# Complex-decay attention ahead of two dense layers: the angle sums and the steps that use them, one slot later

## The chip, the cores and the metric

The kernel runs on one core of a Trainium2 chip. The metric is the device time of one execution in microseconds (us). Before the change it is 1105.33 us, the median of three runs (1104.63 to 1105.64). The core has TensorE (PE in the profile, its weight loads PEld), VectorE (DVE), ScalarE (ACT), GpSimd (POOL) and SyncE (SP), which issues most of the DMAs. Each engine works through its own queue in order.

## The reference

Three stages. The first is a linear attention with a complex decay over 4 batches, 8 heads, 768 steps and head size 48:

```python
mag = sqrt(a_re**2 + a_im**2); a = (a_re + 1j*a_im) * minimum(mag, 0.999) / (mag + 1e-6)
for t in range(768):                                # per batch and head
    S = a[t][:, None] * S + outer(k[t], v[t])       # complex state, real k and v
    y[t] = q[t] @ S.real
```

Then `x = y` as 3072 rows of 384; `h = x @ w_in` (to 2048 columns), `g = h * tanh(softplus(h))`, `x = g @ w_out`; and `out = ((x @ w_a) * (x @ w_b)) @ w_out2` with 1536 columns inside.

## The kernel before

The kernel works in blocks: block j holds the 128 time steps j*128 to j*128+127 of all four batches, that is 512 rows, so there are 6 blocks. The attention works in chunks: chunk c = 4*j + b is 128 steps of one batch with all 8 heads, 24 chunks in all. Chunks 0 to 3 are done in a lead-in of their own. The attention of the later ones is threaded through the first dense stage: while block j goes through `w_in` and `w_out`, the chunks of block j+1 are prepared, so that no attention is left for block 5 and none for the second dense stage.

**The dense work around it.** Lines 913 and following run over units (block, f) with 16 values of f a block. A unit is: nine matmuls into `hps` (`moe1_h`, L594); one or more attention slots; the first half of the activation (`mish_factor`: VectorE L600, then four ScalarE steps on tile `m`, recorded at the helper's L59); nine matmuls of the unit two back into three `x2ps` banks (`moe1_x2`, L637; in block 0 three slower ones on unsplit numbers); one or more slots again; and `mish_product` (VectorE L614, L620, GpSimd L621), which also frees the `hps` bank. There are two `hps` banks, so the `hps` of a unit needs the L614 of the unit two back. From block 2 to block 4 there are 32 slots for the 32 half-units of a block, one each; in block 0 there are 43 and in block 1 there are 44, so some half-units hold two.

**The slots.** Chunk c has its first slot at `slot_0(c)`, 8 slots after that of chunk c-1 (20 after it at chunk 8). The lists `early` and `late` (L551 to L562) give each step a slot relative to it; within a slot the steps with the larger relative number, those of the chunk in front, are written first, and `trig`, `angle` and `decay_exp` ahead of all. So slot 6 of chunk c is also slot 14 of chunk c-1. The steps that matter here, by relative slot:

- 4: `carry` (L302) and `split_theta` (L309): the angles of the chunk get the turn carried over from the chunk four back, and are split into a high part `sh` (GpSimd L316) and a low part `sl` (VectorE L320).
- 5: `sum_ell` (L323): the running sum over time of the logarithms of the decay, a product with a triangular matrix, in a PSUM bank `pl`.
- 6: `sum_theta` (L323, matmuls at L329): the same for the angles, in a bank `pt`, two matmuls; and `decay_exp` (L343): two exponentials on ScalarE that read `pl` (out tile `size`).
- 7: `reduce_angle` (L349): VectorE reads `pt` twice (L353, L354) and works once more on the result in SBUF (L355); `hand_turn` (L359) and `hand_end` (L364) issue a DMA each on SP that carries the chunk's last row to the chunk four later; `scale_qk` (L381).
- 11: `trig`, sine and cosine of the reduced angles on ScalarE; 12: `rotate`.
- 14 and 15: `transposes` (L422) of the first and of the last four heads: four transposes of the queries into a bank `pqT`, four of the keys into `pkT` (L410), each copied out by ScalarE (`qT`, `kT`).
- 16: `scores` (L441): eight heads of products into two banks `psc` (L433), copied with the causal mask by VectorE (L439, `am`); 17: `values` (L445, bank `py`, L463), `outer` (bank `pu`) and `state`.

**The banks.** `pl`, `pqT`, `pkT`, `pt`, `psc`, `py` and `pu` of these chunks share the three PSUM banks of the pool `ps_a` (L116), so each of them needs that the bank of the third one in front, in the order in which they are written, has been read. The order of the ten is: `pl`; `pqT`, `pkT` (first heads, chunk c-1); `pt` (chunk c); `pqT`, `pkT` (last heads, chunk c-1); `psc`, `psc`, `py`, `pu` (chunk c-1). So `pt` takes the bank that `decay_exp` frees.

**The order on an engine.** The program is written in the order above, but the framework places an instruction behind later written ones where its own plan says that it isn't ready yet; the order in the trace is the one that it chose.

Of the kernel before, what the change touches and what calls it, by code (L numbers as in the profile page):

```python
# [21 lines left out]
def kernel(  # L22
# [524 lines left out]
    def slot_0(c):  # L547
# [3 lines left out]
    early = [  # L551
        (-4, load_a), (0, decay_1), (1, decay_2), (1, decay_3), (2, tangent), (2, decay_4), (3, angle),
        (3, split_ell),
        (4, carry), (4, split_theta), (5, sum_ell), (6, sum_theta), (6, decay_exp), (7, reduce_angle),
        (7, hand_turn), (7, hand_end), (7, scale_qk), (11, trig),
    ]
    late = [
        (10, read_end), (11, load_v), (14, lambda c: transposes(c, 0)), (15, lambda c: transposes(c, 1)),
# [597 lines left out]
```

## Time and profile before

| | us |
|---|---|
| median of three runs | 1105.33 (1104.63 to 1105.64) |
| the profiled execution | 1105.48 |
| its span, from the first to the last instruction | 1103.8 |
| PE busy / DVE busy / ACT busy / POOL busy | 1052.8 / 655.9 / 613.8 / 230.0 |

The span is one execution as the hardware profiler recorded it; the rest of the profiled time, 1.7 us, lies around it. A row of a timeline gives start, duration, engine, line, operation, the tile written and the tiles read, the shapes, and in brackets how long the engine had been idle and what ended that. The ends of matmuls are modelled and overlap the next one; the rate of a stretch of matmuls is read from their starts. The attention of chunks 4 to 23 lies between about 60 and 560 us; what follows is dense work alone.

### The profile page before, as it was taken

The page shows a single profiled execution, that of the slowest core. Times are in us where ns is not written, and L with a number is a line of the kernel's source. Part 1 is how long each engine was busy: PE and PEld are TensorE (multiplying, and loading weights), DVE is VectorE, ACT ScalarE, POOL GpSimd, SP SyncE. Part 2 cuts the span into 40 slices and gives each one's busy share as a digit, 9 for nine tenths or more (in the row PEclk, how much of TensorE's full clock was granted, in tenths as well). Part 3 has the DMA queues.
Part 4 walks back from the last instruction along what each step waited for, and adds up shares of the span by engine and source line. Part 5 has one row for each costly group of instructions (what it writes and reads, how often), then busy time and mean ns, then how long its engine had stood idle before and what let it go on. Part 6 is the DMA issues. An engine that isn't in the chain of part 4 may idle for free.

```text
span 1103.8 us, 15912 instructions
## 1 busy us (share of the span) xinstructions
PE 1052.8 (95%) x6060; PEld 875.5 (79%) x6060; DVE 655.9 (59%) x998; ACT 613.8 (56%) x968; POOL 230.0 (21%) x265
## 2 busy tenths in 40 slices
PE   4989989999999999999999999999999999999997
PEld 2856656878887888888777878888888888888886
DVE  6799965787677677676669998641322322322222
ACT  8868876898788887778767853221222212221211
POOL 2012343343334434433331122200000000000000
PEclk9999999999999999999999999999999999999999
DMA  9548752353534343343145457210000100100000
GB/s 203 107 138 197 176 150 61 70 94 74 121 67 86 72 94 66 68 113 79 44 114 179 140 187 226 85 58 1 29 30 1 53 5 1 43 1 1 29 1 31
DMA packets 203549, 90.92 MB, mean 82 GB/s; under 512 B 144781, under 2 KB 187850, under 8 KB 203466
## 3 DMA queue, kind: packets, MB, share of 16 engines
q1 hardware_dynamic: 202410, 89.62, 32.9%
q8 instruction: 50, 0.82, 0.3%
q10 hardware_dynamic: 1056, 0.21, 0.1%
q14 instruction: 33, 0.27, 0.1%
HBM read 72.44 MB, written 17.36 MB: 81 GB/s over the span
## 4 chain that ended last, share of the span: by engine, by line
PE 67%; DVE 13%; ACT 9%; issue 5%; DMA 3%; POOL 2%; SPq 1%; ACTq 0%; DVEq 0%; POOLq 0%
PE ops L717 12%; PE psa L692 12%; PE psb L692 12%; PE x2ps L637 11%; PE hps L594 10%; ACT m L59 4%; PE psc L433 3%; PE py L463 3%; ACT L54 2%; DVE m L600 1%; PE pu L502 1%; PE pkT L410 1%; PE pqT L410 1%; DVE wf L168 1%; DVE wf L169 1%
## 5 line engine op out<-in xcount | busy, mean ns | idle before, releaser
L703 DVE TENSOR_TENSOR a_sb<-a_sb,psb 128x512 f32<-128x512 f32 x72 | 49.3, 685 | 225.0 <-PE psb L692 225.0
L59 ACT ACTIVATE m<-m 128x512 f32<-128x512 f32 x192 | 119.9, 630 | 74.4 <-DVE m L600 63.6
L59 ACT ACTIVATE a_sb<-psa 128x512 f32<-128x512 f32 x72 | 42.9, 595 | 161.5 <-PE psa L692 159.4
L59 ACT ACTIVATE ph<-a_sb 128x512 fp32r<-128x512 f32 x72 | 45.4, 631 | 156.8 <-DVE a_sb L703 156.8
L594 PE MATMUL hps<-xh,winh 128*128 128x512 f32 x288 | 119.2, 415 | 6.3 <-DVE gh L611 5.2
L621 POOL TENSOR_TENSOR gl<-m,gh 128x512 fp32r<-128x512 f32 x64 | 82.9, 1295 | 157.6 <-DVE gh L620 146.0
L594 PE MATMUL hps<-xl,winh 128*128 128x512 f32 x288 | 113.4, 394 | 0.0
L594 PE MATMUL hps<-xh,winl 128*128 128x512 f32 x288 | 113.1, 393 | 0.0
L717 PE MATMUL ops<-woh,ph 128*128 128x384 f32 x288 | 97.2, 337 | 0.0
L717 PE MATMUL ops<-woh,pl 128*128 128x384 f32 x288 | 97.2, 337 | 0.0
L637 PE MATMUL x2ps<-gl,wouth 128*128 128x512 f32 x240 | 94.6, 394 | 2.3 <-DVE gl L621 1.3
L717 PE MATMUL ops<-wol,ph 128*128 128x384 f32 x288 | 96.8, 336 | 0.0
L637 PE MATMUL x2ps<-gh,wouth 128*128 128x512 f32 x240 | 93.8, 404 | 1.8 <-ACT gh L59 1.5
L637 PE MATMUL x2ps<-gh,woutl 128*128 128x512 f32 x240 | 94.0, 392 | 0.0
L614 DVE SCALAR_TENSOR_TENSOR m<-m,hps 128x512 f32<-128x512 f32 x80 | 54.5, 682 | 61.5 <-ACT m L59 61.2
L692 PE MATMUL psa<-xh,wal 128*128 128x512 f32 x216 | 85.2, 395 | 0.0
L692 PE MATMUL psa<-xl,wah 128*128 128x512 f32 x216 | 85.1, 394 | 0.0
L692 PE MATMUL psa<-xh,wah 128*128 128x512 f32 x216 | 84.4, 391 | 0.4 <-DVE a_sb L703 0.4
L692 PE MATMUL psb<-xh,wbh 128*128 128x512 f32 x216 | 84.3, 390 | 0.0
L692 PE MATMUL psb<-xh,wbl 128*128 128x512 f32 x216 | 84.2, 390 | 0.0
L692 PE MATMUL psb<-xl,wbh 128*128 128x512 f32 x216 | 84.2, 390 | 0.0
L600 DVE TENSOR_SCALAR m<-hps 128x512 f32<-128x512 f32 x96 | 65.4, 682 | 17.0 <-PE hps L594 16.7
(167 smaller groups left out, 2324.3 us busy)
## 6 DMA issues: line engine op xcount, KB each, us to landing
wraw<-in_moe_w_out_dram SPq DMA_DIRECT2D x14, 768.0 KB
wraw<-in_moe_w_in_dram SPq DMA_DIRECT2D x8, 768.0 KB
a<-in_a_re_dram SPq DMA_DIRECT2D x24, 192.0 KB
q<-in_q_dram SPq DMA_DIRECT2D x24, 192.0 KB
k<-in_k_dram SPq DMA_DIRECT2D x24, 192.0 KB
v<-in_v_dram SPq DMA_DIRECT2D x24, 192.0 KB
wraw<-in_moe_w_a_dram SPq DMA_DIRECT2D x6, 768.0 KB
wraw<-in_moe_w_b_dram SPq DMA_DIRECT2D x6, 768.0 KB
```

The lines of the kernel that those rows point to most:

```text
L54: load = nc.scalar.preload_act_table_set(name)
L59: x = nc.scalar.activation(**kw)
L433: nc.tensor.matmul(p[:, i, :], lhsT=st["kT", c, hf][:, i, :], rhs=st["qT", c, hf][:, i, :], start=True, stop=True)
L463: nc.tensor.matmul(p[par * 64:(par + 1) * 64, i, :], lhsT=w[:, col:col + 64], rhs=x[:, first + par, :], start=(n == 0), stop=(n == len(ter ...
L594: nc.tensor.matmul(p, lhsT=w[:, kk, :], rhs=x[:, kk, :], start=(i == 0), stop=(i == len(ops) - 1))
L600: nc.vector.tensor_scalar(m, p, 20.0, None, ALU.min)
L614: nc.vector.scalar_tensor_tensor(m, m, 2.5, p, ALU.subtract, ALU.mult)
L621: (nc.vector if on_act else nc.gpsimd).tensor_tensor(gl, m, gh.bitcast(F32), ALU.subtract)
L637: nc.tensor.matmul(x2ps[m], lhsT=w[:, ms], rhs=x, start=(f == 0 and i == 0), stop=(f == NF - 1 and i == len(terms) - 1),)
L692: nc.tensor.matmul(p, lhsT=w[:, kk, :], rhs=x[:, kk, :], start=(i == 0), stop=(i == len(ops) - 1))
L703: nc.vector.tensor_tensor(a_sb, a_sb, pb, ALU.mult)
L717: nc.tensor.matmul(ops_t[t], lhsT=x[:, tsl], rhs=w, start=(f == 0 and i == 0), stop=(f == NF2 - 1 and i == 2),)
```

## The change

Three numbers in the list `early`: `sum_theta` goes from slot 6 to slot 7, `reduce_angle` and `hand_turn` go from slot 7 to slot 8. No instruction is added, removed or altered.

```diff
     early = [
         (-4, load_a), (0, decay_1), (1, decay_2), (1, decay_3), (2, tangent), (2, decay_4), (3, angle),
         (3, split_ell),
-        (4, carry), (4, split_theta), (5, sum_ell), (6, sum_theta), (6, decay_exp), (7, reduce_angle),
-        (7, hand_turn), (7, hand_end), (7, scale_qk), (11, trig),
+        (4, carry), (4, split_theta), (5, sum_ell), (7, sum_theta), (6, decay_exp), (8, reduce_angle),
+        (8, hand_turn), (7, hand_end), (7, scale_qk), (11, trig),
     ]
```

As written, the angle sums of chunk c then stand behind the second transposes of chunk c-1, in front of the next unit's `hps`, and `reduce_angle` and `hand_turn` stand behind the `scores` of chunk c-1. The order of the ten banks becomes `pl`, `pqT`, `pkT`, `pqT`, `pkT`, `pt`, `psc`, `psc`, `py`, `pu`: `pt` now takes the bank of the first `pkT`, and `py` takes the bank of `pt`. The chunks of the lead-in are not touched, since their order is written out apart.

## Rows read from the trace of the kernel before

**Rows 1.** The page's first part: busy time of TensorE.
```profile
PE 1052.8 (95%) x6060; PEld 875.5 (79%) x6060; DVE 655.9 (59%) x998; ACT 613.8 (56%) x968; POOL 230.0 (21%) x265
```
**Rows 2.** Busy time by stretch: PE, PEld, DVE, ACT, POOL, then clock, DMA share, GB/s.
```profile
60.00:130.00 70.00, 63.07 (x440) 42.80 (x439) 67.20 (x100) 55.93 (x88) 14.39 (x16) 1.00 0.68 183
292.00:504.00 212.00, 208.06 (x1462) 173.78 (x1458) 151.36 (x242) 170.41 (x269) 82.09 (x100) 1.00 0.39 85
```
**Rows 3.** Waits of PE: whole span, then 300 to 510: us, times, longest.
```profile
PE pt L329 <- ACT size L59: 6.2, 12, 1.1
...
PE pt L329 <- ACT size L59: 3.9, 9, 0.5
```
**Rows 4.** Timeline of PE, slots 6 to 9 of chunk 16.
```profile
355.39 0.63 PE L410 MATMUL pkT<-ident,khp 128*128 128x128 f32 x4
355.77 0.48 PE L637 MATMUL x2ps<-gh,wouth 128*128 128x512 f32 x1
356.73 0.41 PE L329 MATMUL pt<-sh,csum_r 128*128 128x384 f32 x1 [0.48 <-ACT size L59]
...
357.31 0.39 PE L637 MATMUL x2ps<-gl,wouth 128*128 128x512 f32 x1
...
359.92 0.48 PE L594 MATMUL hps<-xh,winh 128*128 128x512 f32 x1
...
362.07 1.95 PE L433 MATMUL psc<-qT,kT 128*128 128x128 f32 x16
...
366.02 0.44 PE L463 MATMUL py<-qT,W 128*64 128x128 f32 x4
```
**Rows 5.** The same of chunks 14, 22 and 23: first key transposes, next hps.
```profile
305.85 0.63 PE L410 MATMUL pkT<-ident,khp 128*128 128x128 f32 x4
...
310.39 0.48 PE L594 MATMUL hps<-xh,winh 128*128 128x512 f32 x1
...
503.21 0.63 PE L410 MATMUL pkT<-ident,khp 128*128 128x128 f32 x4
...
507.75 0.48 PE L594 MATMUL hps<-xh,winh 128*128 128x512 f32 x1
...
527.62 0.63 PE L410 MATMUL pkT<-ident,khp 128*128 128x128 f32 x4 [0.24 <-DVE khp L395]
...
532.40 0.48 PE L594 MATMUL hps<-xh,winh 128*128 128x512 f32 x1
```
**Rows 6.** The same behind the last chunk, where no angle sums follow.
```profile
551.33 0.63 PE L410 MATMUL pkT<-ident,khp 128*128 128x128 f32 x4
...
554.67 0.47 PE L594 MATMUL hps<-xh,winh 128*128 128x512 f32 x1
```
**Rows 7.** Timeline of PE, chunk 11: angle sums between transposes and hps.
```profile
243.81 0.42 PE L329 MATMUL pt<-sh,csum_r 128*128 128x384 f32 x1
...
244.25 0.39 PE L594 MATMUL hps<-xh,winh 128*128 128x512 f32 x1
```
**Rows 8.** Timeline of ACT, slots 6 and 7 of chunk 16.
```profile
357.57 0.63 ACT L59 ACTIVATE m<-m 128x512 f32<-128x512 f32 x1
358.09 0.60 ACT L59 ACTIVATE kT<-pkT 128x512 f32<-128x512 f32 x1
```
**Rows 9.** Timeline of DVE, slots 6 to 8 of chunk 16.
```profile
357.51 0.56 DVE L353 TENSOR_SCALAR a<-pt 128x384 f32<-128x384 f32 x1 [0.54 <-PE pt L329]
358.10 0.56 DVE L354 TENSOR_TENSOR a<-pt,a 128x384 f32<-128x384 f32 x1
...
359.17 1.08 DVE L355 TENSOR_SCALAR a<-a 128x384 uint32<-128x384 uint32 x1
...
362.10 0.69 DVE L614 SCALAR_TENSOR_TENSOR m<-m,hps 128x512 f32<-128x512 f32 x1 [1.52 <-ACT m L59]
...
363.64 1.36 DVE L439 COPY_PREDICATED am<-csum,psc 128x512 f32<-128x512 int32 x2
```
**Rows 10.** Line 355 from 300 to 510: duration in ns, min/median/max.
```profile
L355 DVE TENSOR_SCALAR a<-a x9: 352/1024/1196, 309.6 to 507.0; 128x384 uint32<-128x384 uint32 x9
```
**Rows 11.** Timeline of POOL beside it.
```profile
359.03 1.00 POOL L384 TENSOR_TENSOR k<-k,size 128x384 f32<-128x384 f32 x1 [0.73 <-DMA k<-in_k_dram]
```

## The prediction, made before the changed kernel ran

> **What bounds the kernel.** I began with the page's busy times: TensorE is busy for 1052.8 us of the span [rows 1], so whatever gives it time shortens the kernel and whatever another engine saves does not, unless TensorE waits for it. I then cut the time into stages. From 292 to 504 us, where the slots come one to a half-unit, TensorE is busy 208.06 of 212.00 us, and ScalarE (170.41) and VectorE (151.36) have room; from 60 to 130 us it is VectorE that is full, 67.20 of 70.00 us [rows 2]. Next I asked what TensorE waits for. The angle sums `pt` stand out: 12 waits, 6.2 us, all for the exponentials that read `pl`, and nine of them, 3.9 us, lie in the even stretch [rows 3]. That idle time is less than what is lost, because a matmul's modelled end covers the start of a gap. So I went to the timeline of one chunk [rows 4]: behind the first key transposes one x2 matmul starts at 355.77, the next thing to start is the angle sum at 356.73, and the second x2 matmul starts only at 357.31. An order that was written ahead of the whole x2 group was put behind its first matmul, and still came too early for ScalarE.
>
> **The sum, part by part.** I measure the stretch from the first key transposes to the next `hps`, because both orders hold the same work in it: four key transposes, nine x2 matmuls, two angle sums, eight second transposes.
>
> Now: 355.39 to 359.92 = 4.53 us [rows 4]; in the first of the nine 310.39 - 305.85 = 4.54, in the last 507.75 - 503.21 = 4.54 [rows 5]. The last chunk has its sums in the same place and is worse: 532.40 - 527.62 = 4.78 [rows 5].
>
> After: behind the last chunk the same stretch runs with no angle sums in it, 554.67 - 551.33 = 3.34 us [rows 6]. What two ready angle sums add between transposes and an `hps` is seen at chunk 11, where the framework happened to put them there: 244.25 - 243.81 = 0.44 us [rows 7]. Together 3.78 us.
>
> Gain: 9 x (4.53 - 3.78) = 6.75 us, and 4.78 - 3.78 = 1.00 us at the last chunk, 7.75 us in all. For this to stand, nothing else may become late by more than it has room. I take the users in the order in which TensorE meets them, at chunk 16, 0.75 us earlier than now:
>
> - The second transposes take the bank of `pl`, free before 356.73 [rows 4], and are reached over 1 us later. The keys among them take the bank of the first `pqT`, whose copy stands in front of that of `kT` on ScalarE. No cost.
> - The angle sums are reached at 355.39 + 3.34 = 358.73 and need the bank of the first `pkT`, copied from 358.09 to 358.69 [rows 8]. That is level. A wait of 0.1 us for each of ten would cost 1 us; none costs 0. I take 0, since the copy is over 0.04 us before, and keep 1 us for the range.
> - The next `hps` is reached at 358.73 + 0.44 = 359.17 and needs the L614 of the unit two back. Its last ScalarE step ends at 357.57 + 0.63 = 358.20 [rows 8]; with 0.69 us for L614 [rows 9] it is free at 358.89. Today L614 shares VectorE with the two reads of `pt` that stand before it. 0.28 us to spare.
> - `py` is reached at 366.02 - 0.75 = 365.27 [rows 4] and needs the masked copies, which end at 363.64 + 1.36 = 365.00 today [rows 9]. They stand behind an L614 that waits for ScalarE until 362.10, so they don't get earlier. 0.27 us to spare, if `reduce_angle` finds its place before 362.10. The angle sums end near 359.2; the reads take 0.56 + 0.56 [rows 9] and L355 0.35 to 1.20 [rows 10], so they are over by 361.5, inside the 1.52 us for which VectorE idles [rows 9] and the place that L355 has now. No cost.
> - `hand_turn` goes behind `hand_end` on SP and waits there for L354. Behind it on SP stand the read of the chunk's end values and the next chunk's carried turn. The first is used at slot 17, the second at the next chunk's slot 4, so a microsecond there is hidden; without that cover it would be one DMA wait a chunk. `trig` comes four slots behind the angle sums, and the split parts `sh` and `sl` are freed a slot later than now but wanted again only at slot 11. Both at no cost, hidden by those slots.
>
> **The uneven part** is chunks 4 to 13, in blocks 0 and 1. There the x2 groups, slots and waits do not repeat. Of the twelve waits nine are in the even stretch and one in the last chunk; the other two lie here and hold less than 6.2 - 3.9 = 2.3 us [rows 3]. In block 0 VectorE is full, so what TensorE gains it would wait off again. Bounds: a gain of 2.3 us, and a loss of the two reads, 1.1 us, at four chunks, 4.5 us. I take 0, as nothing is taken off or put on the full engine.
>
> The sum is made against the profiled execution, 1105.48 us: 1105.48 - 7.75 = 1097.7. The median of the runs is 0.15 lower, so I predict **1097.6 us**. Its own range, with the bounds above, is 1095 to 1103.
>
> **A rule that speaks against it.** L355 took 1.08 us at 359.17, beside a GpSimd product that ran from 359.03 to 360.03 [rows 9, 11], while the shortest of the nine took 0.35 [rows 10]. The Trainium skill, "SBUF — State Buffer", section "Who interferes with whom", says that VectorE and GpSimd share a port pair which one of them holds for a whole instruction while the other stands still. The trace agrees. By that rule the moved L355 could be made to wait for a whole GpSimd operation of the slot that it moves into, ahead of the masked copies; as an estimate that stays under the 1.20 us of the nine, so the sum would not change, but the third rival's chance rises.
>
> **The rivals.**
>
> 1. *The wait changes its place and stays as long.* The bank of `pkT`, the L614 and the masked copies all hang on ScalarE's steps, and the room is 0.0, 0.3 and 0.3 us. If ScalarE or VectorE has its steps in another order so that one of the three comes 0.75 us later, `py` starts at 366.02 again: 1105. For it: the small margins. Against: today's order of ScalarE doesn't depend on `pt` in this stretch, and each margin is counted with nothing moved forward. If half goes, the time is near 1101.5.
> 2. *The change does not do what it says.* The framework orders by its own plan, so the sums could land at a wrong place again. TensorE always has an `hps` or x2 matmul ready, though, and the sums are now written behind both the x2 group and the transposes, so they can't come in front of these unless those are not ready in its plan. 1105, a small chance.
> 3. *Slower: `reduce_angle` lands between the L614 of 362.10 and the masked copies.* It is written behind `scores`, and `py` now takes the bank of `pt` as well, so either way `py` waits for both. Price: 0.56 + 0.56 + 0.35 to 1.20 = 1.47 to 2.32 us behind 365.00, so `py` starts at 366.5 to 367.3, that is 0.45 to 1.3 us later than today, at ten chunks 4.5 to 13 us: 1110 to 1118, middle 1114. It decides as soon as the reads start behind 361 us on this clock. For it: the program order, and the margin of 0.27 us. Against: the sums are ready 2 us and more before the scores are, with VectorE idle in between.
>
> **The chances.** The forecast 0.62, half of it 0.08, no gain (rivals 1 and 2, the loss in the uneven part eating the gain) 0.14, slower 0.16. A measurement of this kernel tells 0.2%, about 2.2 us, from no change. Faster by more than that is 0.62 + 0.08 = 0.70, within it 0.14, slower 0.16. The range 1094 to 1107.5 holds the forecast, the half and no gain; most of rival 3 lies outside.
>
> **What would show it.** Right: in the changed trace the angle sums stand behind eight second transposes in chunks 14 to 23, with no wait for the exponentials; key transposes to `hps` takes some 3.8 us; `py` to `py` of neighbouring chunks falls by 0.75 us; L353 starts near 359.4 on this clock, before an L614. Wrong: the sums wait for the copy of `kT`; `py` waits for `am`; L353 stands behind that L614; or the even stretch gains and the time before 292 us loses as much.

## The result, and the profile after

The changed kernel takes **1092.31 us**, the median of four runs (1091.60 to 1092.88), beside 1104.98 us (1104.04 to 1105.64) for the kernel before on the same chip: a ratio of 0.989, 95% interval 0.9876 to 0.9905. It is 12.67 us faster, where 7.75 had been forecast, and ends below the low end of the range, which the prediction gives once as 1095 and once as 1094 us. Its profiled execution took 1092.23 us, with a span of 1090.4 us, 13.4 less than before.

Where the 13.4 us come from is read off the start of the first `py` matmul of a chunk (us from the start of the span), in the timelines of PE of both kernels:

| | before | after | gained since the row above |
|---|---|---|---|
| `py` of chunk 4 | 94.30 | 93.61 | 0.69 |
| `py` of chunk 7, the last prepared during block 0 | 167.90 | 162.89 | 4.32 |
| `py` of chunk 12 | 291.62 | 286.25 | 0.36 |
| `py` of chunk 23 | 560.77 | 547.48 | 7.92 |
| end of the span | 1103.8 | 1090.4 | 0.11 |

The last eleven chunks give 7.92 us, which is what the sum of 7.75 was about. The other 5.5 us were gained ahead of that nearly all, 5.0 of them by the end of block 0, for which the prediction had put down 0.

Not all of these 5.0 us are the change's. Before the first step that it moves, the angle sums of chunk 4 at about 60 us, the two profiles already lie apart: `pl` of that chunk starts at 60.12 us before and at 57.41 after. TensorE's granted clock was 0.66 from 50 to 60 us in the profile before, at the end of the lead-in, and 1.00 in the profile after. It is a matter of the single execution: the same kernel before, profiled once more (e0 below), kept its clock. The stretch in the first profile and in e0:

```profile
50.00:60.00 10.00, 10.00 (x65) 7.77 (x65) 8.38 (x14) 6.54 (x9) 1.30 (x2) 0.66 0.44 115
...
50.00:60.00 10.00, 9.77 (x101) 7.40 (x100) 8.84 (x14) 8.07 (x13) 1.51 (x2) 1.00 0.43 120
```

At the third unit's `hps` (65.69 us before, 64.04 after) 1.65 us of that are left. Without them the profiles lie some 11.8 us apart, and block 0 gains 5.0 - 1.65 = 3.4 us.

**The even stretch.** Busy time by stretch, kernel after (columns as in [rows 2]):

```profile
292.00:500.00 208.00, 207.46 (x1434) 175.64 (x1433) 152.31 (x245) 172.25 (x277) 83.16 (x99) 1.00 0.39 84
```

TensorE idles 0.54 us in 208, where it idled 3.94 in 212. The view of PE's waits over the whole span, kernel after, no longer has a row of `pt` for the tile `size` [rows 3]; this is all that `pt` waits for on ScalarE now, in the lead-in:

```profile
PE pt L329 <- ACT a L59: 5.3, 2, 2.8
```

Timeline of PE, slots 6 to 9 of chunk 16, kernel after, against [rows 4]:

```profile
348.81 0.63 PE L410 MATMUL pkT<-ident,khp 128*128 128x128 f32 x4
...
351.35 0.60 PE L410 MATMUL pqT<-ident,qhp 128*128 128x128 f32 x4
...
352.26 0.42 PE L329 MATMUL pt<-sh,csum_r 128*128 128x384 f32 x1
...
352.68 0.39 PE L594 MATMUL hps<-xh,winh 128*128 128x512 f32 x1
...
358.69 0.44 PE L463 MATMUL py<-qT,W 128*64 128x128 f32 x4
```

The angle sums stand where they were written, behind the second transposes. From the first key transposes to the next `hps` it is 352.68 - 348.81 = 3.87 us, 0.66 less than the 4.53 of before; 3.78 had been forecast. The bank that `pt` takes comes from a key copy that ScalarE ends at 351.51 + 0.60 = 352.11, in its timeline of the same slots:

```profile
351.51 0.60 ACT L59 ACTIVATE kT<-pkT 128x512 f32<-128x512 f32 x1
```

`pt` starts 0.15 us behind that. It was said to be level with it, and about 0.1 us goes there. In eight of the ten chunks it is the same 0.14 to 0.15 us; in the two others, where the copy ended 0.33 and 0.38 us ahead, nothing is lost. It comes back: the nine `hps` matmuls in front of the scores now start 0.23 us apart with no gap, so that from this `py` to the next chunk's it is 382.75 - 358.69 = 24.06 us, where it was 24.77.

VectorE in the same slots, kernel after, against [rows 9]:

```profile
353.44 0.55 DVE L353 TENSOR_SCALAR a<-pt 128x384 f32<-128x384 f32 x1
...
354.61 0.50 DVE L355 TENSOR_SCALAR a<-a 128x384 uint32<-128x384 uint32 x1
...
356.71 0.74 DVE L439 COPY_PREDICATED am<-csum,psc 128x512 f32<-128x512 int32 x1
...
357.68 0.73 DVE L439 COPY_PREDICATED am<-csum,psc 128x512 f32<-128x512 int32 x1
```

The reads of `pt` are over before the masked copies begin. They start 353.44 - 348.81 = 4.63 us behind the first key transposes, where 359.4 - 355.39 = 4.01 had been forecast: a step that the prediction left out, VectorE's L620, stands in front of them and took 1.14 us here, beside a GpSimd product of 1.02, where it takes 0.43 in other chunks. The masked copies end at 358.41, 0.28 us ahead of `py`, and 9.60 us behind the first key transposes, as before (365.00 - 355.39 = 9.61).

**Block 0.** What was lost there before, and isn't after, is a wait of TensorE. It stood in the view of PE's waits of the kernel before:

```profile
PE py L463 <- DVE am L439: 5.2, 1, 5.2
```

PE's timeline of the kernel before, the place of this wait, and the busy time by stretch behind it (clock in the third column from the right):

```profile
140.33 0.44 PE L463 MATMUL py<-qT,W 128*64 128x128 f32 x4
145.98 0.69 PE L463 MATMUL py<-am,v 128*64 128x128 f32 x4 [5.21 <-DVE am L439]
...
149.01 1.17 PE L502 MATMUL pu<-v,khp 128*64 128x48 f32 x28
...
146.00:149.00 3.00, 3.00 (x28) 3.00 (x30) 0.98 (x2) 3.00 (x5) 2.09 (x2) 0.50 0.60 225
```

The same place in PE's timeline of the kernel after:

```profile
140.74 0.44 PE L463 MATMUL py<-qT,W 128*64 128x128 f32 x4
...
142.54 1.09 PE L502 MATMUL pu<-v,khp 128*64 128x48 f32 x32
```

The products of this chunk, chunk 6, took 149.01 - 140.33 = 8.68 us before and take 1.80 after. Only 5.21 of the 6.88 us are the wait itself. Behind it the `py` groups of four matmuls, seven from the start of that row to `pu`, take (149.01 - 145.98)/7 = 0.43 us each in place of (142.54 - 140.74)/8 = 0.22; the granted clock was 0.50 from 146 to 149 us. Some 1.5 us are what the wait cost on top, in clock.

Why the masked copies were late is seen on VectorE, kernel before:

```profile
132.99 1.90 DVE L383 TENSOR_TENSOR q<-q,size 128x384 f32<-128x384 f32 x1
134.81 2.24 DVE L355 TENSOR_SCALAR a<-a 128x384 uint32<-128x384 uint32 x1
136.97 2.17 DVE L384 TENSOR_TENSOR k<-k,size 128x384 f32<-128x384 f32 x1
139.06 2.55 DVE L168 SCALAR_TENSOR_TENSOR wout<-wraw,wout 128x768 uint32<-128x768 uint32 x1
141.65 2.44 DVE L169 SCALAR_TENSOR_TENSOR wout<-wraw,wout 128x768 uint32<-128x768 uint32 x1
...
145.21 1.33 DVE L439 COPY_PREDICATED am<-csum,psc 128x512 f32<-128x512 int32 x2
```

and on GpSimd beside it, kernel before, where line 179 subtracts the high part of a weight tile from the whole:

```profile
132.62 1.85 POOL L179 TENSOR_TENSOR winl<-wf,winh 128x768 fp32r<-128x768 f32 x1 [6.85 <-ACT winh L59]
134.42 2.17 POOL L179 TENSOR_TENSOR woutl<-wout,wouth 128x768 fp32r<-128x768 f32 x1
...
136.86 6.41 POOL L179 TENSOR_TENSOR woutl<-wout,wouth 128x768 fp32r<-128x768 f32 x3
```

Five VectorE instructions in a row that work on SBUF alone take 1.9 to 2.6 us each, 11.3 us together, while GpSimd runs five subtractions with one short memset between. After, the same stretch of VectorE, and GpSimd's first subtraction beside it, read:

```profile
130.35 0.94 DVE L168 SCALAR_TENSOR_TENSOR wout<-wraw,wout 128x768 uint32<-128x768 uint32 x1
131.33 2.49 DVE L169 SCALAR_TENSOR_TENSOR wout<-wraw,wout 128x768 uint32<-128x768 uint32 x1
133.74 2.17 DVE L384 TENSOR_TENSOR k<-k,size 128x384 f32<-128x384 f32 x1
135.82 0.55 DVE L353 TENSOR_SCALAR a<-pt 128x384 f32<-128x384 f32 x1
136.40 0.56 DVE L354 TENSOR_TENSOR a<-pt,a 128x384 f32<-128x384 f32 x1
137.00 0.79 DVE L355 TENSOR_SCALAR a<-a 128x384 uint32<-128x384 uint32 x1
...
138.90 1.34 DVE L439 COPY_PREDICATED am<-csum,psc 128x512 f32<-128x512 int32 x2
...
129.25 3.75 POOL L179 TENSOR_TENSOR winl<-wf,winh 128x768 fp32r<-128x768 f32 x1 [4.20 <-ACT winh L59]
```

With the angle sums a slot later, the reads L353 and L354, which had begun at 131.6, stand behind L168 and L169, the decoding of `w_out`, which had been the end of the row. L168 runs unstretched; here it is GpSimd's first subtraction that takes 3.75 us in place of 1.85. Two VectorE instructions are stretched in place of five, and the masked copies start 6.3 us earlier. What this is worth, by the waits of TensorE: between 120 and 170 us the one of 5.2 and one of 1.1 for `size` are gone, with 1.5 us of clock; four new waits, three of them for ScalarE, bring 1.3, 0.7, 0.7 and 0.5 us. 7.8 - 3.2 = 4.6 us, beside the 4.32 of the table for chunks 4 to 7; 1.0 us is lost again ahead of chunk 4 (1.65 - 0.69), to which a section below comes back.

### The profile page after: what moved, and what is told of

Read it like the earlier page. It is cut to its first block, busy times and chain, and to the rows that moved or that the text cites. A ratio compares the mean times of both kernels' runs of the same rounds, so it can differ in the third digit from the quotient of the medians.

```text
span 1090.4 us, 15921 instructions
## 1 busy us (share of the span) xinstructions
PE 1048.8 (96%) x6060; PEld 874.0 (80%) x6060; DVE 653.7 (60%) x998; ACT 611.5 (56%) x968; POOL 232.0 (21%) x265
## 4 chain that ended last, share of the span: by engine, by line
PE 70%; DVE 13%; ACT 6%; issue 5%; DMA 3%; POOL 2%; SPq 1%; ACTq 0%; DVEq 0%; POOLq 0%
PE ops L717 12%; PE psb L692 12%; PE psa L692 12%; PE x2ps L637 12%; PE hps L594 11%; PE psc L433 3%; PE py L463 3%; ACT m L59 3%; PE pkT L410 2%; DVE wf L168 1%; PE pqT L410 1%; ACT L54 1%; DVE wf L169 1%; DVE m L600 1%; DVE wf L167 1%
## 5 line engine op out<-in xcount | busy, mean ns | idle before, releaser
L621 POOL TENSOR_TENSOR gl<-m,gh 128x512 fp32r<-128x512 f32 x64 | 83.2, 1300 | 151.9 <-DVE gh L620 131.6
L705 DVE TENSOR_TENSOR pl<-a_sb,ph 128x512 fp32r<-128x512 f32 x72 | 52.2, 726 | 39.0 <-ACT ph L59 39.0
```

Source lines behind the costliest of these rows:

```text
L621: (nc.vector if on_act else nc.gpsimd).tensor_tensor(gl, m, gh.bitcast(F32), ALU.subtract)
L705: nc.vector.tensor_tensor(lo, a_sb, hi.bitcast(F32), ALU.subtract)
```

## The experiments

They ran in four batches, each on a chip of its own: e1 to e4; e0 and e5 to e7; e8 to e10; e11. The kernel before takes 1102.2 to 1103.0 us there, some 2 us less than on the first chip, and each ratio is against its runs in the same batch. An expectation in us that was counted from the first chip is to be read with that. The columns behind the ratio come from one profiled execution each: the start of `py` of chunk 4, and the time from `py` of one chunk to that of another.

| run | us | ratio (95%) | chunk 4 | 4 to 7 | 7 to 8 | 12 to 23 |
|---|---|---|---|---|---|---|
| before, first profile | 1104.98 | | 94.30 | 73.60 | 42.02 | 269.15 |
| after, first profile | 1092.31 | 0.989 (0.9876 to 0.9905) | 93.61 | 69.28 | 42.21 | 261.23 |
| e0, before again | 1100.9, one run | | 93.04 | 71.63 | 42.04 | 269.19 |
| e1, sums alone | 1091.63 | 0.9894 (0.988 to 0.9909) | 92.61 | 71.56 | 42.02 | 261.03 |
| e2, reduce and hand alone | 1099.77 | 0.9967 (0.9955 to 0.998) | 96.00 | 69.50 | 42.05 | 269.23 |
| e3, from chunk 8 on | 1093.88 | 0.9918 (0.9905 to 0.9931) | 92.61 | 73.66 | 42.03 | 261.02 |
| e4, up to chunk 7 | 1100.04 | 0.9973 (0.9963 to 0.9984) | 94.69 | 69.72 | 42.03 | 269.54 |
| e5, before, subtractions in written place | 1103.52 | 1.001 (1.0002 to 1.0019) | 93.22 | 66.40 | 47.57 | 269.15 |
| e6, after, the same | 1094.63 | 0.9929 (0.9916 to 0.9942) | 94.38 | 65.34 | 46.23 | 261.02 |
| e7, after, reads behind the masked copies | 1093.22 | 0.9911 (0.9897 to 0.9925) | 94.67 | 68.42 | 42.04 | 262.11 |
| e8, after, subtractions tied | 1089.49 | 0.9878 (0.9862 to 0.9893) | 96.06 | 66.02 | 42.02 | 261.16 |
| e9, before, subtractions tied | 1096.43 | 0.9944 (0.9931 to 0.9958) | 92.69 | 67.63 | 42.06 | 269.24 |
| e10, after again | 1090.99 | 0.9897 (0.988 to 0.9913) | 94.49 | 68.54 | 42.07 | 261.15 |
| e11, from chunk 8 on, subtractions tied | 1087.81 | 0.987 (0.9853 to 0.9886) | 92.64 | 67.65 | 42.04 | 261.01 |

### The change taken apart

**e1** moves the sums alone, **e2** the other two steps alone:

```diff
-        ... (6, sum_theta), ...
+        ... (7, sum_theta), ...                            # e1
-        ... (7, reduce_angle),
-        (7, hand_turn), ...
+        ... (8, reduce_angle),                             # e2
+        (8, hand_turn), ...
```

> Only the angle sums move (slot 7); the reduction of the angles and its DMA stay in slot 7, behind them. Theory A (two gains: about 7.9 us in the even stretch because TensorE no longer waits at the sums, and about 5.4 us in block 0 because VectorE has fewer instructions that stand still beside GpSimd ahead of the masked copies of chunk 6): both come with the sums, since the reduction follows them anyway: 1092 to 1093 us, the wait of py for am in block 0 gone. Rival B (the reduction's own slot is what relieves VectorE in block 0): 1097 to 1098 us, the wait of about 5 us for am still there. Third rival of the prediction (reduction ahead of the masked copies is what matters in the even stretch): no statement here.

> Only the reduction and its DMA move (slot 8); the angle sums stay in slot 6. Theory A: nothing in the even stretch, 24.8 us from py to py as before, and in block 0 at most the part that the reduction has in it: 1102 to 1105 us. Rival B: about 5 us of gain in block 0, 1099.5 to 1100.5 us.

The sums alone give the whole of 12 to 23, 261.03 us, and the whole of the time, 0.9894. The two other steps alone give nothing there, 269.23. Their slot is without effect in the even stretch, then: `reduce_angle` follows its sums wherever it is written. In block 0 each half by itself takes the 5.2 us wait away or shortens it: e2 has none, e1 has 1.7 us for the masks and 1.2 for L354. So theory A was right on the even stretch, but not on e2: at 1099.77 us it gains 3.0 us, none of it in the even stretch, and lies where rival B had it.

**e3** and **e4** make the change for one part of the chunks:

```diff
+            if fn in (sum_theta, reduce_angle, hand_turn) and c >= 2 * B:    # e3; e4: c < 2 * B
+                r += 1
```

> The whole change, for chunks 8 to 23 alone; block 0 is ordered as before. Theory A: 7.9 us of gain, all of it behind 292 us, and the wait of py for am of about 5 us near 140 us still there: 1097 us. Rival C (the extra gain is spread over blocks 0 and 1 and comes with the order there as a whole): 1094 to 1096 us.

> The whole change, for chunks 4 to 7 alone. Theory A: the gain of block 0 alone, 5.4 us, and the even stretch as before at 24.8 us from py to py: 1099.5 us; added to the gain of the run from chunk 8 on it makes the whole 12.7 us. Rival C: less than 3 us of gain here, 1102 us or more.

Against the 1102.77 us of the kernel before in this batch, e3 gains 8.9 us and e4 2.7. The two parts add to 11.6, about what the whole change gains in another batch (11.8, e10). Counted as gains from the first chip's 1105 us, theory A had 7.9 for e3 and 5.4 for e4, rival C 9 to 11 and less than 3. e3 lies between them, and e4's 2.7 is rival C's; but block 1, over which rival C spread the gain, has none of it in the columns 7 to 8 (42.0 in all four). e3 keeps a wait of 5.2 us for the masks in block 0; in e4 it is gone, and 1.1 us for the masks of chunk 5 is left. So of the gain that the sum didn't hold 2.7 us come with the order of chunks 4 to 7, and have nothing to do with the order around the `pt` of the even stretch.

### What stretches VectorE in block 0

**e0** is the kernel before once more.

> The kernel before, once more with a profile on the chip of the experiments, where its median was about 2 us lower than where the change was measured. If the 2 us lie in the lead-in and the start of block 0 (py of chunk 4 at 92.6 us as in the run that changes chunks 8 to 23 alone, against 94.3), they have nothing to do with the change; the wait of py for am near 140 us should be there with about 5 us, and 24.8 us from py to py in the even stretch.

Program and order on VectorE are the same as in the first profile, but four instructions are stretched in place of five (L384, which fell beside a GpSimd memset there, took 0.55 us), and the wait for the masks is 3.4 us in place of the 5 that were expected. `py` of chunk 4 starts at 93.04 us, 1.3 earlier than in the first profile, as the third unit's `hps` does (64.35): that is the lead-in's clock. How the two engines meet differs between executions of one program; 4 to 7 took 71.6 us here, 73.6 there.

**e5** keeps the eight subtractions for the split `w_out`, which is used from block 1 on, in the place where they are written, in block 1, where the framework had drawn them ahead; **e6** does the same to the changed kernel. Nothing is tied on VectorE. (A dependency of the class `no_sync` sets the order on an engine and adds no wait.)

```diff
-            nc.gpsimd.tensor_tensor(lo, f[0], hi.bitcast(F32), ALU.subtract)
+            pool_ops = [y for y in nc.cur_bb.bb.instructions if y.engine == mybir.EngineType.Pool]
+            x = nc.gpsimd.tensor_tensor(lo, f[0], hi.bitcast(F32), ALU.subtract)
+            if late:
+                tc.add_manual_dep(x.ins, pool_ops[-1].name, no_sync, ...)
```

> The kernel before, with the eight GpSimd subtractions that make the low part of w_out kept in their written place (block 1) instead of running one after another beside chunk 7's slots 6 to 9; VectorE's order in block 0 is as before, instruction by instruction. Theory A (VectorE stands still beside these subtractions, and the masked copies queue behind it): the wait of py for am goes, and 3 to 5 us with it: 1098 to 1100 us where the kernel before takes 1102.8; L383, L355, L384, L168 and L169 near 133 to 144 us, 1.9 to 2.6 us each before, take 0.4 to 1.0. Rival D (it is VectorE's own load and order, GpSimd does not matter): the wait stays, 1102 to 1104 us.

> The changed kernel with the same subtractions kept in their place. Theory A: the gain of the even stretch stays and what the change had won from VectorE in block 0 is won this way as well, with what stayed beside GpSimd (L169 2.49 us, L384 2.17 us): 1089 to 1092 us. Rival D: as the changed kernel, 1091 to 1093 us; over 1093 us if the subtractions hurt in block 1, where GpSimd has other work.

In e5 VectorE has the order of before, and the wait for the masks is gone: 4 to 7 takes 66.40 us. The stretched instructions hang on the subtractions. But 7 to 8 takes 47.57 us in place of 42.0, and 8 to 12 83.37 in place of 81.2, so the time, 1103.52 us, is that of before, where theory A had 1098 to 1100: it was right on the wait and wrong on the time. From 180 to 212 us TensorE is idle for 4.85 us, in the stretch that answers to it before (188 to 220) for 1.67. By itself this couldn't tell a gain in block 0 from a debt that is always paid. e6 goes the same way: 4 to 7 in 65.34, 7 to 8 in 46.23, and with 1094.63 us it is slower than the changed kernel, where theory A had 1089 to 1092; the "over 1093" that was kept for a loss in block 1 came.

**e9** and **e8** find the subtractions a place between: behind the clearing of chunk 8's `v`, which GpSimd does at about 142 us, once the products of chunk 6 are done, and ahead of block 1. e9 is the kernel before with this tie, e8 the changed one, **e10** the changed one itself.

```diff
-            nc.gpsimd.tensor_tensor(lo, f[0], hi.bitcast(F32), ALU.subtract)
+            x = nc.gpsimd.tensor_tensor(lo, f[0], hi.bitcast(F32), ALU.subtract)
+            if late:
+                lows.append(x)
...                                    # one that is written behind the clearing gets the same tie
-        nc.gpsimd.memset(t[:, H * D:], 0.0)
+        x = nc.gpsimd.memset(t[:, H * D:], 0.0)
+        if c == 2 * B:
+            for y in lows:
+                tc.add_manual_dep(y.ins, x.ins.name, no_sync, ...)
```

> The kernel before, its sums in the old slot, with the same tie of the eight subtractions; VectorE's order in block 0 stays as it was. Theory A: no wait of py for the masks, py of chunk 4 to py of chunk 7 in 66 to 68 us in place of 71.6 to 73.6, and less than 2 us of that given back in block 1: 1097 to 1100.5 us, the block-0 part of the change's gain without the change; 12 to 23 stays at 269.2. Rival B: the time is given back in block 1 in full, 1102 to 1104 us, no gain.

> The changed kernel, and the eight GpSimd subtractions of block 1's wout kept back until the GpSimd memset of chunk 8's v (about 142 us), behind the last masked copies and angle reductions of block 0 and ahead of block 1. Theory A (in block 0 the gain is VectorE freed of the stretch beside GpSimd's subtractions; keeping them too long is paid in block 1): the stretched VectorE instructions between 131 and 139 us go back to 0.4 to 1.0 us each, py of chunk 4 to py of chunk 7 takes 65 to 67 us in place of 69.3, block 1 loses under 1.5 us, 12 to 23 stays at 261.0: 1089 to 1091.5 us. Rival B (wherever GpSimd's work stands, what it takes from VectorE comes out the same): 1091.5 to 1094 us, as the changed kernel.

> The changed kernel itself beside the two, so that they are compared on one chip with the same runs of the kernel before. Both theories: 1090.5 to 1092.5 us, 0.9885 to 0.991 of the kernel before; py of chunk 12 to py of chunk 23 in 261.0 to 261.3 us. How py of chunk 4 to py of chunk 7 comes out against the 69.3 us of the first profile tells how much that stretch differs between executions of one program.

e9 is 6.4 us faster than the kernel before without the change, 1096.43 us, 0.6 below the 1097 to 1100.5 of theory A, and far from rival B. Its VectorE, in the stretch and the order of the kernel before (line numbers of these kernels are nine higher), and GpSimd beside it:

```profile
131.37 1.88 DVE L392 TENSOR_TENSOR q<-q,size 128x384 f32<-128x384 f32 x1
133.17 0.35 DVE L364 TENSOR_SCALAR a<-a 128x384 uint32<-128x384 uint32 x1
133.44 0.55 DVE L393 TENSOR_TENSOR k<-k,size 128x384 f32<-128x384 f32 x1
133.91 0.95 DVE L169 SCALAR_TENSOR_TENSOR wout<-wraw,wout 128x768 uint32<-128x768 uint32 x1
134.89 0.96 DVE L170 SCALAR_TENSOR_TENSOR wout<-wraw,wout 128x768 uint32<-128x768 uint32 x1
...
136.97 1.34 DVE L448 COPY_PREDICATED am<-csum,psc 128x512 f32<-128x512 int32 x2
...
131.00 1.83 POOL L180 TENSOR_TENSOR winl<-wf,winh 128x768 fp32r<-128x768 f32 x1 [6.86 <-ACT winh L59]
...
141.71 4.33 POOL L180 TENSOR_TENSOR woutl<-wout,wouth 128x768 fp32r<-128x768 f32 x2
```

The same five instructions take 4.69 us in place of 11.30. The one that is still stretched is the one beside the `winl` subtraction, which was left where it was. The Trainium skill, "SBUF — State Buffer", section "Who interferes with whom", says that VectorE and GpSimd share a pair of ports, held for a whole instruction while the other engine stands still, and that a VectorE instruction with at most one input in SBUF, outside its faster two-port modes, doesn't take part. The trace agrees: of the instructions beside GpSimd's run in the changed kernel, L353 and L354, which read `pt` in PSUM, took 0.55 and 0.56 us, as ever, while L384 with two inputs in SBUF took 2.17.

The changed kernel gains from the same tie, 1089.49 (1088.91 to 1089.78) beside 1090.99 us (1090.42 to 1092.22) for e10. That is 1.5 us where the kernel before gains 6.4: the change had taken most of this loss away by chance of order. The profile of e8 has 4 to 7 in 66.02 us, as theory A had it, but `py` of chunk 4 at 96.06. Of the 1.6 us to e10's 94.49, 1.3 are the lower clock of the lead-in again (0.66 from 50 to 60 us, third unit's `hps` at 65.59 and 64.30); the rest of the way to e11 is the subject of the next section.

### The price of the change ahead of chunk 4

**e11** gives block 0 its old slots back, as e3 does, and has the tie of e8 and e9.

> The new slots from chunk 8 on alone, block 0 in its old order, and the eight GpSimd subtractions kept back until chunk 8's v. It puts together the two gains that were measured apart: the even stretch (12 to 23 in 261.0 to 261.2 us in place of 269.2) and block 0 freed of the subtractions with the old slots (py of chunk 4 to py of chunk 7 in 66 to 68 us). Theory A (two separate gains; in block 0 the later sums themselves bring nothing, and cost 1.5 to 2 us ahead of chunk 4, where py of chunk 4 started at 94.5 and 96.1 us in the two last runs with later reads and at 92.7 us with the old slots): py of chunk 4 at 92.4 to 93.2, 1087 to 1089.5 us, 0.985 to 0.988 of the kernel before. Rival B (the later sums in block 0 are worth something beside the tie): 1089.5 to 1092 us.

It takes 1087.81 us (1087.19 to 1088.17), the lowest of all, 0.987 of the kernel before, inside theory A's bounds. The ratio alone doesn't set it apart from e8, whose 0.9878 lies in its interval. `py` of chunk 4 is at 92.64, 4 to 7 in 67.65, 12 to 23 in 261.01. What the change costs ahead of chunk 4 is seen in PE's timelines. First e10, with the busy time of a stretch behind (clock third from the right):

```profile
77.96 0.79 PE L594 MATMUL hps<-xh,winh 128*128 128x512 f32 x1 [4.12 <-DVE gh L611]
...
81.97 1.18 PE L329 MATMUL pl<-size,csum 128*128 128x384 f32 x2
...
78.00:82.00 4.00, 4.00 (x10) 3.13 (x11) 3.97 (x7) 3.96 (x7) 0.60 (x1) 0.50 0.55 188
```

and PE of e11:

```profile
70.24 0.50 PE L605 MATMUL hps<-xh,winh 128*128 128x512 f32 x1 [1.30 <-DVE gh L622]
...
76.79 0.50 PE L605 MATMUL hps<-xh,winh 128*128 128x512 f32 x1 [1.61 <-DVE gh L622]
...
78.97 0.81 PE L338 MATMUL pl<-size,csum 128*128 128x384 f32 x2
...
86.00 0.50 PE L605 MATMUL hps<-xh,winh 128*128 128x512 f32 x1 [1.05 <-DVE gh L622]
```

VectorE is full here in both, and TensorE waits for it as long in both between the first weights and chunk 4: four waits of 1.30, 1.61, 1.05 and 0.76 us and one of 1.26 make 5.98 in e11, one of 4.12, one of 0.76 and one of 1.05 make 5.93 in e10. In one piece, though, the wait is followed by the lower clock, 0.50 or 1.2 GHz from 78 to 82 us: nine `hps` matmuls take 81.97 - 77.96 = 4.01 us in place of 2.18. The difference, 1.83, is about that of the two starts of chunk 4, 94.49 - 92.64 = 1.85, of which 0.30 had been there at the third unit (64.30 and 64.00).

It is the later reads that do this, and not the later sums. The same `hps` in e2 (reads later, sums not) and in e1 (sums later, reads not), and in e1 a stretch of block 0:

```profile
79.16 0.79 PE L594 MATMUL hps<-xh,winh 128*128 128x512 f32 x1 [4.11 <-DVE gh L611]
...
76.78 0.50 PE L594 MATMUL hps<-xh,winh 128*128 128x512 f32 x1 [1.66 <-DVE gh L611]
...
141.00:144.00 3.00, 2.86 (x28) 2.87 (x30) 0.70 (x2) 3.00 (x6) 2.46 (x3) 0.50 0.95 338
```

All seven profiles with the later reads in block 0 have the one wait here (2.55 us in the first profile of the changed kernel, 4.06 to 4.12 in the others), and the seven with the old reads have it in pieces of at most 1.7 us. Pieces don't always spare the clock: e1's waits of 1.18 and 1.66 us for `py` of chunk 6 end 2.1 us apart, and the clock behind them was 0.50 (the last row).

### Does `py` need the bank of `pt`?

The third rival rested on it. **e7** is the changed kernel with the first read of `pt` tied behind the masked copies of the chunk in front, from chunk 14 on, the order in which that rival saw the loss.

```diff
-        nc.vector.tensor_scalar(t[:, 1], pt, MAGIC, MAGIC, ALU.add, ALU.subtract)
+        x = nc.vector.tensor_scalar(t[:, 1], pt, MAGIC, MAGIC, ALU.add, ALU.subtract)
+        if c >= 14:
+            tc.add_manual_dep(x.ins, st["cp", c - 1].ins.name, no_sync, ...)
...
-        nc.vector.copy_predicated(scored(c)[hf], causal, st.pop(("psc", c, hf)))
+        st["cp", c] = nc.vector.copy_predicated(scored(c)[hf], causal, st.pop(("psc", c, hf)))
```

> The changed kernel with the first read of the angle sums tied behind the masked copies of the chunk in front on VectorE, from chunk 14 on. The prediction's third rival as it was priced (1.47 to 2.32 us behind the copies): py to py 25.2 to 26.1 us, 1104 to 1113 us. My reading now: py waits only for the two reads of the bank, 1.12 us less the 0.27 us to spare, 0.85 us at ten chunks: py to py 24.9 us, 1100 to 1101 us. If the place on VectorE does not matter: 1091 to 1093 us.

VectorE of e7 in the slots of chunk 16, and the first `py` matmul beside it on PE:

```profile
357.76 0.73 DVE L441 COPY_PREDICATED am<-csum,psc 128x512 f32<-128x512 int32 x1
358.39 0.54 DVE L353 TENSOR_SCALAR a<-pt 128x384 f32<-128x384 f32 x1
358.96 0.56 DVE L356 TENSOR_TENSOR a<-pt,a 128x384 f32<-128x384 f32 x1
...
358.79 0.44 PE L465 MATMUL py<-qT,W 128*64 128x128 f32 x4
```

The reads do stand behind the copies, and `py` starts at 358.79, before the second read of `pt` has begun. So it isn't in that bank in e7; in which bank `py` is in the changed kernel itself no run shows. From the `py` in front to this one it stays at 24.02 us: neither the third rival's 25.2 to 26.1 nor the author's own 24.9 came. e7 takes 1093.22 us, 0.2 above the 1091 to 1093 that were given for a place that doesn't matter. Over 12 to 23 it is 1.0 us longer than e10, in pieces of 0.2 to 0.4 us at three places, which were not followed up.

## Why the prediction was wrong, and where it was right

**The sum of the even stretch was right.** It gave 7.75 us; 12 to 23 gave 7.92 in the first profiles and 8.0 to 8.2 in e1, e3 and e10. The 0.1 us wait of `pt` for a key copy, kept as a bound of 1 us, is there, and is given back in front of the scores. e1 and e2 show that the sums alone make it. No cost of `hand_turn` behind `hand_end` is seen: e1 without its move is as fast as the whole change.

**The step that failed is the uneven part**: "I take 0, as nothing is taken off or put on the full engine", with a gain of at most 2.3 us as its bound. That bound counted only the waits of `pt`. It took for granted that where VectorE is full its work is a fixed amount, which can't change if no instruction is added. It isn't fixed: the same five instructions took 11.3 us beside GpSimd's subtractions and 4.7 away from them (e9), and moving the sums and the reads altered which VectorE instructions met them. The 5.2 us wait of `py` for the masks was in the same view as [rows 3], and following it to VectorE would have shown the row of stretched instructions. What the change would do to that order couldn't be read from the profile, but a bound on the gain of 5.2 us, the wait, or 6.7 with its clock, could have been. The prediction had the effect itself in hand: it weighed the rule on ports for one L355 in the even stretch, where it mattered for 0.7 us, and not for the stretch where VectorE was full. Its size is known roughly. The medians leave 12.67 - 7.92 = 4.75 us beside the even stretch, and 11.8 - 8.0 = 3.8 with e10; the first profiles have 3.4 us in block 0, with 1.65 more from the lead-in's clock, which is luck and not the change; e4, the change in block 0 alone, gains 2.7.

**The margins in the even stretch were right** to 0.1 us, but for the reads of `pt`. On the clock of the first key transposes `pt` was said to start at 3.34 us and did at 3.45, `hps` at 3.78 and did at 3.87; the masked copies were to end 0.27 us ahead of `py`, and end 0.28 ahead. The reads start at 4.63 where 4.01 was said, behind the L620 that the prediction left out, and L355 is over at 6.30 where 6.11 was the bound; that cost nothing, as the copies come later still. The room of 0.28 us is counted to the first `py` group, which doesn't read the masked copies: in block 0 of the kernel before it started 5.65 us ahead of the group that does. Whether the copies would be the next limit no run shows.

**The third rival's mechanism didn't act where it was tried.** The account that `py` takes the bank of `pt`, and that each bank is the third one in front, came from counting banks in turn. In e7 `py` ran with the second read of `pt` still to come. In block 0 of e1, however, `py` did wait 1.2 us for L354, so which bank a tile gets isn't fixed by the count: it has to be looked up for the chunk in question. The chance of a loss, 0.16, rested on it. The first rival's small margins held: `pt` starts 0.15 us behind the end of the key copy, and the 0.1 us of it that is lost is all. The second didn't happen; the sums stand where they were written.

**What stays open.** Why the framework lays VectorE's order in block 0 as it does for each slot of the sums wasn't tried apart. That the earlier `w_out` decoding is what spares the changed kernel is read from the trace and fits e8, where the tie brings only 1.5 us; no run moved that decoding alone. The gain of block 0 also differs between executions of one program (71.6 and 73.6 us for 4 to 7 of the kernel before), so its share is known to about 2 us only. Why the clock of the lead-in falls in some executions (the first profile of the kernel before, e2 and e8) and not in others is open too.

## What to carry to other kernels

Where an engine is full, count its time from what stands beside it, not from its instructions: look for rows of one line that take two to six times as long as elsewhere, and see what GpSimd does at that time; a long run of GpSimd work there is worth moving to a stretch with room (6.4 us here, more than half of what the change brought), but the place matters: moved a block on, where GpSimd's other work is, it gained nothing (e5). Go through every long wait of the bounding engine before giving a stretch a price of zero, and bound an unknown by those waits and not by the one that the change is aimed at. A long wait can cost more than its length, since the clock may fall behind it; several short ones some microseconds apart, of the same sum, didn't have that cost here (e11), while two that ended 2.1 us apart did (e1). Look at several executions before putting a microsecond or two down to a change: a lower clock in the lead-in moved single profiles by some 1.5 us.

## What the runs showed of the hardware

- VectorE instructions on SBUF alone, of 0.35 to 0.96 us, took 1.9 to 2.6 us beside a GpSimd subtraction of 128x768; those that read PSUM kept their 0.55. Which of the two engines loses differs: in the changed kernel one GpSimd subtraction took 3.75 us for 1.85, and the L168 beside it kept its 0.94.
- The same program had this meeting come out differently in two executions: waits of 5.2 and 3.4 us for the same tile.
- After a wait of 4.12 us TensorE ran at the lower clock (0.50 granted, 78 to 82 us), nine matmuls in 4.01 us for 2.18; with waits of 1.05 to 1.61 us in its place, more than 6 us apart, the granted clock stayed at 1.00 there. Waits of 1.18 and 1.66 us that ended 2.1 us apart (e1) were followed by 0.50 as well.
